# P times V of every fourth key tile as three f16 products, with P split into f16 halves on Pool

## The chip, the cores and the metric

One core of a Trainium2 chip runs the whole layer. The metric is the device time of one launch in microseconds; a smaller one is better. The core has a matrix engine (TensorE, PE in the profile; its weight loads are listed apart as PEld), a vector engine (VectorE, DVE), a scalar engine with activation functions (ScalarE, ACT), a general engine (GpSimd, POOL) and an engine that issues transfers (SyncE, SP). Each runs its own list of instructions in order, and waits on semaphores for the others. Matmul results go to PSUM, of which the kernel uses eight banks of 128 x 512 f32.

## The reference

A transformer block over S = 2048 rows of D = 512, in f32. `mod` holds six rows, `c` being a single conditioning vector.

```python
mod = (_silu(c) @ w_mod).reshape(c.shape[0], 6, 1, -1)
sa, ca, ga, sb, cb, gb = ...
h = _layernorm(x, axis=-1) * (1 + ca) + sa
x = x + ga * _A_ref(h, A_wq, A_wk, A_wv, A_wo)      # 32 query heads of 16, one key and one value head
h = _layernorm(x, axis=-1) * (1 + cb) + sb
x = x + gb * _B_ref(h, B_w_gate, B_w_up, B_w_down)  # ((h Wg) * (h Wu)) Wd, F = 1792
```

In the attention, scores = q k / 4, p = softmax(scores) over 2048 keys, and o = p v. No mask is used.

## The kernel before, in words

**Units and turns.** Attention is cut into 32 units: 8 strips of 256 rows times 4 groups of 8 heads. A unit runs through 16 key tiles of 128 keys. For a key tile, four score products (`qk_exp`, L659, or L657 where the product is issued in two pieces of 256) give 128 keys x 512 (two heads times 256 rows) in a PSUM bank each; ACT takes the exponential of each into an f32 tile P (L661). The row maximum that the exponent needs is folded into the products as an extra row of q, and comes from a separate pass one unit earlier (`max_mm`: products `mx`, L601, reduced by DVE, L605). So in each turn PE makes four products `sc` for ACT and four products `mx` for DVE.

**P times V.** `pv(u, kt)` (L670) multiplies the four P tiles of a key tile by `vst[:, kt, :]`: 16 columns of V, and 16 of ones that sum the softmax. The four products use 32 columns of the array each and run side by side; all are f32. They go to one bank for the 16 key tiles of a unit, which `pv_out` scales and copies out (L676). `end_turn` issues the burst for the key tile of the turn before, so that each turn ends in one burst of four f32 products.

**Side work.** All other products are f16. Where f32 accuracy is wanted, an operand is split into a high and a low f16 half, and three products (high x high, low x high, high x low: `TERMS`) are summed. Score products, maxima and side products use only half of the array's rows, and run in pairs on the two halves. The side work is the q projection (`q_proj`), the output projection (`wo_work`), gate and up (112 groups, 14 for each strip), and down (two groups for each strip). `attend` orders a pair of turns by a string: `NO_SIDE` where no side work is open, `FEW` (four side steps per turn) in the q projections of the first units, and `MANY` (eight per turn) later: x is a step of side work, m a maximum, e a score product, and the figure is the half of the array. The burst and the ends follow the string.

**The guard.** In one turn all side steps use one half of the array, in the next turn the other, but both halves of a group add into one PSUM bank. `Group.half` therefore puts a dependence on the first side step of a turn: it waits for the exponential that followed the last side step of the turn before (`sync`). In `MANY` the last score product comes after the last side step, so that this is the fourth exponential of the turn; and the side step that waits is the first product of the new turn, in front of all others on PE's queue.

**Pool's work.** Pool splits operands into f16 halves: the two halves of the gate-up product after each group (L850, L851), the attention output (L706 to L709), and h2T (L818, L819). Up to some 474 us it also scales and splits the FFN weights, one slice per 1.25 turns or so: three instructions each (L1079 to L1081 for gate and up, L1073, L1080, L1081 for down). `hooks` hands them out by a count of steps, two to a turn, not by Pool's progress.

Of the kernel before, what the change touches and what calls it, by code (L numbers as in the profile page):

```python
# [33 lines left out]
ROW_LAG = 4  # L34
SLOTS = (0, 1, 2, 3, 6, 7)
SUM_GAP = 4.0
# [4 lines left out]
NORM_AT = (5, 12, 15, 19)  # L41
NBANK = 8
QPRE = 24
Q_LAG = 8
# [19 lines left out]
def adaln_mqa_glu_kernel(ctx: ExitStack, tc: tile.TileContext, x_in, wq_in, wk_in, wv_in, wo_in,  # L64
# [160 lines left out]
    hfs = kwb[:, 0:2 * NHF * BT].bitcast(F32).rearrange("p (n t) -> p n t", n=NHF)  # L225
    ssqs = [kwb[:, 2 * n * BT:2 * n * BT + 2 * F].bitcast(F32) for n in (KC, 2 * KC)]
    kng = kwb[:, 2 * NHF * BT:2 * NHF * BT + BT]

# [85 lines left out]
    def v_mm(b):  # L314
        p = ps_hold("pvt", (128, 4, 16))
        for i in range(4):
            nc.tensor.matmul(p[:, i, :], parts[b][:, i * 128:(i + 1) * 128], lane[:, 16:32], start=True, stop=True)

        def out():
            nc.scalar.activation(vst[:, 4 * b:4 * b + 4, 0:16], p, AF.Copy, scale=inv[:, 0:1] if b else 1.0)  # L320
            ps_give(p)
        posts.append(out)
# [47 lines left out]
    q_part(0, 0)  # L370
    kb = consts.tile([128, 8], F32, name="kb")
    inv = consts.tile([128, 3], F32, name="inv")
    fwd = consts.tile([128, 3], F32, name="fwd")
# [13 lines left out]
    nc.vector.tensor_scalar(hsb, modT[0][:, :, 0:64:32], fwd[:, 0:1], None, op0=OP.mult)  # L387
    nc.gpsimd.tensor_scalar(sckb, sck, inv[:, 0:1], 0.0, op0=OP.mult, op1=OP.add)
    combine(0, selk)
    combine((0, 0), selq)  # L390
# [7 lines left out]
    ln_norm(1, (None, nc.scalar, None, nc.scalar))  # L398
    evs = consts.tile([128, 1], F32, name="evs")

    def ev_scales():

        t = work.tile([128, 2], F32, name="evt", bufs=1)
        nc.vector.tensor_reduce(evs, ident.rearrange("p (a r) -> p a r", a=4)[:, :, 0:16], axis=AX.XY, op=OP.add)
        nc.vector.reciprocal(t[:, 0:1], kb[:, 5:6])
        nc.gpsimd.tensor_tensor(t[:, 0:1], t[:, 0:1], evs, op=OP.mult)
        nc.gpsimd.tensor_scalar(t[:, 1:2], evs, -1.0, 1.0, op0=OP.mult, op1=OP.add)
        nc.gpsimd.tensor_tensor(evs, t[:, 0:1], t[:, 1:2], op=OP.add)

    qvs = consts.tile([128, 1], F32, name="qvs")  # L410
# [42 lines left out]
    def last_rows():  # L453
# [20 lines left out]
             12: lambda: (k_evac(3), h_halves(3, KA)), 13: lambda: h_halves(3, KB),  # L474
             15: lambda: h_halves(1, KA), 17: lambda: h_halves(1, KB), 20: ev_scales}
    later_h = deque((2, k) for k in range(KC))
# [164 lines left out]

    pvb = {}
    ptl = {}
    oc = {}
    och = {}
    pd = {}

    def qk_exp(u, kt, p, a, last=False):
        s = sst[u % 3]
        ptl[u, kt, p, a] = work.tile([128, D], F32, name="P", tag="P", bufs=8)  # L650
        t = ps_sc()
# [6 lines left out]
        else:  # L658
            nc.tensor.matmul(t.rearrange("k (c n) -> k c n", c=2), keys, s[64 * a:64 * a + 50, :, p, :],  # L659
                             start=True, stop=True)  # L660
        ex = nc.scalar.activation(ptl[u, kt, p, a], t, AF.Exp)  # L661
        if sync["due"]:
            sync.update(due=False, exp=ex.ins.name)

    def pv(u, kt):
        if kt == 0:
            pvb[u] = ps_hold("pv")
        for j in range(4):
            p, a = divmod(j, 2)
            nc.tensor.matmul(pvb[u][32 * j:32 * j + 32, :], vst[:, kt, :], ptl[u, kt, p, a],  # L670
                             start=(kt == 0), stop=(kt == KT - 1))
# [120 lines left out]
    def ln2_work(sb):  # L792
        st = {}

        def tr(i):
            def f():
                if not h2s:
                    h2T = big.tile([128, 2, 2, KC, ST], F16, name="h2T", tag="wq")
                    glus.append(big.tile([128, 2, 2, FT, ST], F16, name="glu", tag="big"))
                    h2s.update({s: h2T[:, s % 2] for s in range(NS)})  # L800
# [31 lines left out]
    def ffn_work(sb):  # L832

        def glu():
            return glus[0][:, sb % 2]

# [56 lines left out]
    def late_weights():  # L893
# [37 lines left out]
        def stage(n):  # L931
            if "d" in W:
                t = work.tile([128, D], F32, name="wsl", tag="xl", bufs=3)
            else:
                t = hfs[:, SLOTS[taken[0] % len(SLOTS)], :]
                taken[0] += 1
# [281 lines left out]
    def attend(u, kt):  # L1218
# [6 lines left out]
        style = NO_SIDE if side is None else FEW if side in few else MANY  # L1225
        orders = [[(w[0], int(w[1:] or 0)) for w in s.split()] for s in (style if style is NO_SIDE else (style, style))]
        count = {}

        def end_turn(kt):
# [3 lines left out]
            for f in ends:  # L1233
                f()
            ends.clear()
            v = u * KT + kt - 1
# [76 lines left out]

    pv(u, KT - 1)
    pv_out(u)
    sync["before"] = sync["exp"]
# [60 lines left out]
```

## Time and profile before

| what | value |
|---|---|
| median of three runs | 1665.11 us (1664.57 to 1665.29) |
| span of the profiled execution | 1663.8 us |
| PE busy | 1643.3 us, 99% of the span |
| DVE busy | 1402.3 us, 84% |
| ACT busy | 1234.8 us, 74% |
| POOL busy | 523.5 us, 31% |

The profiled execution has only a span, from the first to the last instruction; it is 1.3 us below the median of the timed runs. A row of the timeline gives the start, the length, the engine, the line, the operation, the tiles (out<-in), how many instructions the row merges, and in brackets how long the engine sat idle before it, and what ended that. A row of the groups gives after the count the busy time of the group and the mean length of one instruction in ns. A row of the windows gives for each engine the busy us and in brackets the number of instructions, and then the granted TensorE clock as a share of full speed.

### The profile page before, as it was taken

Reading aid. Unit: us, or ns where it says so; the run is one execution under the profiler, and the core shown is the slowest. Engines: PE = TensorE matmul, PEld = TensorE weight load, DVE = VectorE, ACT = ScalarE, POOL = GpSimd, SP = SyncE. Lnnn points to the kernel's source line nnn. Section 1 sums busy time; section 2 is a strip of 40 time slices with the busy share of each in tenths; the row PEclk is TensorE's granted clock in tenths of the full one; section 3 lists DMA queues with packets and bytes.
Section 4 is the critical chain, followed back from the end, with each engine's and each line's share of the span. In section 5 each row is a group of like instructions: output and inputs, shape, how many; then the busy total and the mean of one; then the engine's idle time right before and its main releaser. Section 6 shows DMA issues by size and latency. Waiting matters only on the chain.

```text
span 1663.8 us, 39821 instructions
## 1 busy us (share of the span) xinstructions
PE 1643.3 (99%) x15677; PEld 747.1 (45%) x15677; DVE 1402.3 (84%) x2434; ACT 1234.8 (74%) x2389; POOL 523.5 (31%) x833
## 2 busy tenths in 40 slices
PE   8899999999999999999999999999999999999999
PEld 4333333355533554335543355434545345454776
DVE  7999999998998999899998999999998999980211
ACT  5688888888777877777877787777878777877300
POOL 4857537864841111301112011300113001210322
PEclk9999999999999999999999999999999999999999
DMA  6313313342210001000000000000000000000100
GB/s 237 108 59 100 95 43 120 96 129 80 77 51 24 18 12 32 19 32 20 20 26 23 25 13 24 26 25 26 20 29 15 26 22 20 26 14 21 33 13 14
DMA packets 66024, 75.39 MB, mean 45 GB/s; under 512 B 17702, under 2 KB 46634, under 8 KB 65836
## 3 DMA queue, kind: packets, MB, share of 16 engines
q1 hardware_dynamic: 63724, 72.26, 13.7%
q8 instruction: 123, 2.02, 0.5%
q10 hardware_dynamic: 2112, 0.59, 0.1%
q14 instruction: 65, 0.53, 0.1%
HBM read 55.51 MB, written 17.04 MB: 44 GB/s over the span
## 4 chain that ended last, share of the span: by engine, by line
PE 93%; ACT 2%; DVE 2%; DMA 1%; issue 1%; POOL 0%; SPq 0%; ACTq 0%; DVEq 0%
PE side L511 41%; PE pv L670 30%; PE mx L601 8%; PE sc L659 8%; PE sc L657 3%; ACT P L661 2%; DVE mpart L605 1%; DMA xbig<-in_A_x_dram 1%; PE mx L805 1%; PE mxt L629 0%; ACT hf L813 0%; PE sc L601 0%; DVE bs L248 0%; DMA kwb<-in_B_w_down_dram 0%; DMA wkv<-in_A_wv_dram 0%
## 5 line engine op out<-in xcount | busy, mean ns | idle before, releaser
L605 DVE TENSOR_REDUCE mpart<-mx 128x1 f32<-128x512 f32 x2016 | 1274.1, 684 | 104.0 <-PE mx L601 95.7
L661 ACT ACTIVATE P<-sc 128x512 f32<-128x512 f32 x2048 | 1094.8, 598 | 274.2 <-PE sc L659 226.9
L601 PE MATMUL mx<-kst,sst 48*128 48x512 f16 x2032 | 631.5, 377 | 3.8 <-ACT P L661 1.7
L659 PE MATMUL sc<-sst,kst 50*128 50x512 f16 x1792 | 597.5, 379 | 0.6 <-ACT P L661 0.3
L670 PE MATMUL pv<-P,vst 128*32 128x512 f32 x4096 | 545.3, 605 | 0.7
L511 PE MATMUL side<-h2T,wg 64*128 64x256 f16 (+1 forms) x2396 | 540.8, 271 | 0.1
L511 PE MATMUL side<-h2T,wu 64*128 64x256 f16 (+1 forms) x2396 | 538.7, 270 | 0.0
L511 PEld LDWEIGHTS <-wg 64*128 64x128 f16 (+1 forms) x2396 | 226.0, 94 | 230.5 <-ACT P L661 194.0
L511 PE MATMUL side<-wd,glu 64*128 64x512 f16 (+1 forms) x1172 | 272.8, 378 | 0.2 <-ACT P L661 0.2
L850 POOL TENSOR_SCALAR glu<-gf 128x256 f16<-128x256 f32 x112 | 45.8, 409 | 671.3 <-DVE gf L849 583.9
L511 PEld LDWEIGHTS <-wu 64*128 64x128 f16 (+1 forms) x2396 | 226.4, 94 | 43.0 <-issue 7.8
L601 PEld LDWEIGHTS <-sst 48*128 48x128 f16 x2064 | 189.9, 94 | 34.2 <-issue 17.4
L659 PEld LDWEIGHTS <-kst 50*128 50x128 f16 x1792 | 162.9, 94 | 63.0 <-issue 50.3
L511 PEld LDWEIGHTS <-glu 64*128 64x128 f16 (+1 forms) x1172 | 98.5, 94 | 192.4 <-ACT P L661 85.9
L670 PEld LDWEIGHTS pv<-P,vst 128*32 128x32 f32 x4096 | 80.7, 108 | 160.9 <-issue 150.1
L849 DVE TENSOR_TENSOR gf<-side,g 128x256 f32<-128x256 f32 x112 | 46.7, 418 | 79.8 <-ACT g L847 77.7
L657 PE MATMUL sc<-sst,kst 50*128 50x256 f16 x512 | 96.9, 268 | 0.1
L511 PE MATMUL side<-h,wq 64*128 64x512 f16 (+1 forms) x372 | 95.0, 376 | 0.4 <-ACT P L661 0.4
L847 ACT ACTIVATE g<-side 128x256 f32<-128x256 f32 x112 | 42.3, 379 | 65.6 <-PE side L511 65.3
L511 PE MATMUL side<-wo,och 64*128 64x512 f16 (+1 forms) x360 | 86.3, 377 | 0.0
L851 POOL TENSOR_TENSOR glu<-gf,glu 128x256 f16<-128x256 f32 x112 | 75.3, 673 | 9.3
L706 POOL TENSOR_TENSOR oc<-oc,rr 128x256 f32<-128x256 f32 x31 | 22.7, 731 | 146.6 <-DMA rr<-ri 100.4
(233 smaller groups left out, 865.4 us busy)
## 6 DMA issues: line engine op xcount, KB each, us to landing
pd<-ev SPq DMA_DIRECT2D x32, 256.0 KB
kwb<-in_B_w_gate_dram SPq DMA_DIRECT2D x32, 224.0 KB
kwb<-in_B_w_up_dram SPq DMA_DIRECT2D x32, 224.0 KB
sst<-qd SPq DMA_DIRECT2D x180, 32.0 KB
qd<-q SPq DMA_DIRECT2D x16, 256.0 KB
oc<-pd SPq DMA_DIRECT2D x64, 64.0 KB
rr<-ri SPq DMA_DIRECT2D x64, 64.0 KB
x<-in_A_x_dram SPq DMA_DIRECT2D x14, 256.0 KB
```

The lines of the kernel that those rows point to most:

```text
L511: return nc.tensor.matmul(self.p[:, c * w:(c + 1) * w], left[rows], right[rows], start=start and c == 0, stop=stop and c == len(terms) - 1)
L601: nc.tensor.matmul(m, s[64 * a:64 * a + 48, t // 2, p, t % 2 * 128:(t % 2 + 1) * 128], w[64 * a:64 * a + 48, :], start=(i == 0), stop=(i = ...
L605: nc.vector.tensor_reduce(part, m, axis=AX.X, op=OP.max)
L657: nc.tensor.matmul(t[:, c * ST:(c + 1) * ST], keys, s[64 * a:64 * a + 50, c, p, :], start=True, stop=True)
L659: nc.tensor.matmul(t.rearrange("k (c n) -> k c n", c=2), keys, s[64 * a:64 * a + 50, :, p, :], start=True, stop=True)
L661: ex = nc.scalar.activation(ptl[u, kt, p, a], t, AF.Exp)
L670: nc.tensor.matmul(pvb[u][32 * j:32 * j + 32, :], vst[:, kt, :], ptl[u, kt, p, a], start=(kt == 0), stop=(kt == KT - 1))
L706: eng.tensor_tensor(o, o, st["r"], op=OP.mult)
L847: nc.scalar.activation(g, p[:, 0:ST], AF.Copy, scale=2.0 ** -45)
L849: nc.vector.tensor_tensor(gf, p[:, ST:2 * ST], g, op=OP.mult)
L850: nc.gpsimd.tensor_scalar(glu()[:, 0, f, :], gf, 1.0, 0.0, op0=OP.mult, op1=OP.add)
L851: nc.gpsimd.tensor_tensor(glu()[:, 1, f, :], gf, glu()[:, 0, f, :], op=OP.subtract)
```

## The change

In `MANY` turns, every fourth key tile (kt = 0, 4, 8, 12) is now a split tile, once the space for it exists (it lies behind the gate-up halves, in a place that is free from the sixth unit on). Its four P tiles are written into one of two sets; Pool makes a high and a low half of each (`p_halves`, two instructions per P tile, one P tile per turn, at the turn's end); and its part of P times V is three f16 products for each P tile, with V split once into `v16`. The burst of a split tile is kept back until the next split tile is due, which is four turns later. At the end of a unit, what is kept back follows the last f32 burst at once. To keep P and V in the range of f16, all exponentials now get a bias of 14 ln 2 from a 128 x 1 tile (`pbias`), and V is scaled by `vsc` when it is stored; the scaling in `pv_out` falls away. The gate-up halves have one buffer instead of two, and two of the six staging slots of the weights lie elsewhere.

```diff
-SLOTS = (0, 1, 2, 3, 6, 7)
+SLOTS = (0, 1, 2, 3, 12, 13)
+EVERY = 4
+P_BIAS = float(14 * np.log(2.0))
...
+    pbias = consts.tile([128, 1], F32, name="pbias")
+    nc.gpsimd.memset(pbias, P_BIAS)
+    v16 = consts.tile([128, 2, KT // EVERY, 32], F16, name="v16")
...
     def qk_exp(u, kt, p, a, last=False):
...
-        ptl[u, kt, p, a] = work.tile([128, D], F32, name="P", tag="P", bufs=8)
+        if (u, kt) in split_p:
+            ptl[u, kt, p, a] = p_sets[split_p[u, kt]][0][:, 2 * a + p]
+            todo_p.append((u, kt, p, a))
+        else:
+            ptl[u, kt, p, a] = work.tile([128, D], F32, name="P", tag="P", bufs=8)
...
-        ex = nc.scalar.activation(ptl[u, kt, p, a], t, AF.Exp)
+        ex = nc.scalar.activation(ptl[u, kt, p, a], t, AF.Exp, bias=pbias)
...
+    def p_halves():
+        if todo_p:
+            u, kt, p, a = todo_p.popleft()
+            hi, lo = p_view(split_p[u, kt], 2 * a + p)
+            t = ptl[u, kt, p, a]
+            nc.gpsimd.tensor_scalar(hi, t, 1.0, 0.0, op0=OP.mult, op1=OP.add)
+            nc.gpsimd.tensor_tensor(lo, t, hi, op=OP.subtract)
+
     def pv(u, kt):
...
+        for n, (vl, pl) in enumerate(((0, 0), (1, 0), (0, 1))):
+            for j in range(4):
+                p, a = divmod(j, 2)
+                nc.tensor.matmul(pvb[u][32 * j:32 * j + 32, :], v16[:, vl, kt // EVERY, :],
+                                 p_view(split_p[u, kt], 2 * a + p)[pl], start=start and n == 0, stop=stop and n == 2)
+
+    def pv_turn(u, kt):
+        if (u, kt) in split_p:
+            late_p.append((u, kt))
+            if len(late_p) > 1:
+                pv(*late_p.popleft())
+        else:
+            pv(u, kt)
+        if kt == KT - 1:
+            while late_p:
+                pv(*late_p.popleft())
+            ends.append(lambda: pv_out(u))
...
-        nc.scalar.activation(ev, pvb[u], AF.Copy, scale=evs)
+        nc.scalar.activation(ev, pvb[u], AF.Copy)
...
+        if style is MANY and kt % EVERY == 0 and p_sets:
+            split_p[u, kt] = len(split_p) % 2
...
         def end_turn(kt):
...
+            p_halves()
             v = u * KT + kt - 1
             if v >= 0:
-                pv(*divmod(v, KT))
-                if v % KT == KT - 1:
-                    ends.append(lambda: pv_out(u - 1))
+                pv_turn(*divmod(v, KT))
```

In the built program 105 of the 512 key tiles are split tiles, the first of them the last of the sixth unit, and Pool has 420 pairs of new instructions. Three places show how the instructions move.

On Pool, in the sixth unit, where the first split tile comes. `kwb`, `wu` and `wg` are the FFN weights being split, `gf` a gate-up product, and `glu` is the tile that holds both the gate-up halves and, new, the P sets. Before:

```order
L1079 TENSOR_SCALAR kwb<-kwb,sca 128x448
L1080 TENSOR_SCALAR wu<-kwb 128x448
L1081 TENSOR_TENSOR wu<-kwb,wu 128x448
L1079 TENSOR_SCALAR kwb<-kwb,sca 128x448
L1080 TENSOR_SCALAR wu<-kwb 128x448
L1081 TENSOR_TENSOR wu<-kwb,wu 128x448
L1079 TENSOR_SCALAR kwb<-kwb,sca 128x448
```

and now, from the same first row on:

```order
L1129 TENSOR_SCALAR kwb<-kwb,sca 128x448
L1130 TENSOR_SCALAR wu<-kwb 128x448
L1131 TENSOR_TENSOR wu<-kwb,wu 128x448
L680 TENSOR_SCALAR glu<-glu 128x512
L681 TENSOR_TENSOR glu<-glu 128x512
L680 TENSOR_SCALAR glu<-glu 128x512
L681 TENSOR_TENSOR glu<-glu 128x512
L1129 TENSOR_SCALAR kwb<-kwb,sca 128x448
L1130 TENSOR_SCALAR wu<-kwb 128x448
L1131 TENSOR_TENSOR wu<-kwb,wu 128x448
L680 TENSOR_SCALAR glu<-glu 128x512
L681 TENSOR_TENSOR glu<-glu 128x512
```

One pair L680, L681 now stands in Pool's queue for every turn from here to the last unit's end, between the slices of the weights, which keep their places by steps.

On PE, at the end of a unit (`sc` is a score product, `side` a side group, here of gate and up). Before, the burst is four f32 products, and the first weight load of the next turn waits for ACT:

```order
L657 MATMUL sc_5277<-sst0_128,kst_132 128x256
L670 MATMUL pv_4542<-P_5154,vst_126 32x512
L670 MATMUL pv_4542<-P_5198,vst_126 32x512
L670 MATMUL pv_4542<-P_5168,vst_126 32x512
L670 MATMUL pv_4542<-P_5220,vst_126 32x512
L511 LDWEIGHTS wg_4055 [waits Activation_49]
```

and now twelve f16 products stand behind the four, of which these are the first:

```order
L667 MATMUL sc_5276<-sst0_128,kst_132 128x256
L692 MATMUL pv_4541<-P_5151,vst_126 32x512
L692 MATMUL pv_4541<-P_5197,vst_126 32x512
L692 MATMUL pv_4541<-P_5165,vst_126 32x512
L692 MATMUL pv_4541<-P_5219,vst_126 32x512
L700 LDWEIGHTS v16_341
L700 MATMUL pv_4541<-glu_4878,v16_341 32x512 [waits Pool_49]
```

The f16 products wait for Pool. They end as the f32 ones do, in front of a weight load that waits for ACT.

On PE, one turn later (the turn of kt = 1 of a unit): the burst that stood there is gone, and the weight load that waits for ACT follows the score product directly.

```order
L509 LDWEIGHTS wu_4055
L509 MATMUL side_5202<-h2T_4877,wu_4055 128x256
L667 LDWEIGHTS kst_132
L667 MATMUL sc_5341<-sst0_128,kst_132 128x256
L509 LDWEIGHTS wg_4054 [waits Activation_49]
L509 MATMUL side_5202<-h2T_4877,wg_4054 128x256
```

More of the change, by code (lines that the diff above doesn't have):

```diff
@@ L319, in out @@
         def out():
-            nc.scalar.activation(vst[:, 4 * b:4 * b + 4, 0:16], p, AF.Copy, scale=inv[:, 0:1] if b else 1.0)
+            nc.scalar.activation(vst[:, 4 * b:4 * b + 4, 0:16], p, AF.Copy, scale=vsc[:, 1:2] if b else vsc[:, 0:1])
             ps_give(p)
@@ L388, in adaln_mqa_glu_kernel @@
     nc.gpsimd.tensor_scalar(sckb, sck, inv[:, 0:1], 0.0, op0=OP.mult, op1=OP.add)
+    nc.vector.reciprocal(vsc[:, 0:1], kb[:, 5:6])
+    nc.gpsimd.tensor_tensor(vsc[:, 1:2], vsc[:, 0:1], inv[:, 0:1], op=OP.mult)
     combine(0, selk)
@@ L398, in adaln_mqa_glu_kernel @@
     ln_norm(1, (None, nc.scalar, None, nc.scalar))
[L399 to L408, printed above, removed]
     qvs = consts.tile([128, 1], F32, name="qvs")
@@ L642, in adaln_mqa_glu_kernel, with p_view @@
     pvb = {}
+    did_pv = {}
     ptl = {}
+    split_p = {}
+    p_sets = []
+    todo_p = deque()
+    late_p = deque()
+    def p_view(n, j):
+        return [p_sets[n][1][:, j, h] for h in range(2)]
     oc = {}
```

41 lines of the change are left out of this document (29 added, 12 removed).

## The prediction

> **What bounds the kernel now.** I read the page first, then the groups, then the timeline of single turns, and last Pool by windows.
>
> ```profile
> span 1663.8 us, 39821 instructions
> PE 1643.3 (99%) x15677; PEld 747.1 (45%) x15677; DVE 1402.3 (84%) x2434; ACT 1234.8 (74%) x2389; POOL 523.5 (31%) x833
> POOL 4857537864841111301112011300113001210322
> PE 93%; ACT 2%; DVE 2%; DMA 1%; issue 1%; POOL 0%; SPq 0%; ACTq 0%; DVEq 0%
> L661 ACT ACTIVATE P<-sc 128x512 f32<-128x512 f32 x2048 | 1094.8, 598 | 274.2 <-PE sc L659 226.9 <-PE mx L601 30.6 <-PE side L511 3.1
> L670 PE MATMUL pv<-P,vst 128*32 128x512 f32 x4096 | 545.3, 605 | 0.7
> ```
>
> PE is busy throughout and carries 93% of the chain that ended last, so whatever shortens or lengthens PE's list moves the end. Pool's 31% is a mean over unlike stages: in the first eleven slices (to 458 us) it stands at 3 to 8 tenths, afterwards mostly at 1.
>
> Two turns in the timeline, one with side steps of down and one of gate and up, show how close ACT runs behind PE:
>
> ```profile
> 900.77 1.06 PE L670 MATMUL pv<-P,vst 128*32 128x512 f32 x8
> 901.77 0.39 PE L511 MATMUL side<-wd,glu 64*128 64x512 f16 x1
> 902.00 0.38 PE L511 MATMUL side<-wd,glu 64*128 64x512 f16 x1
> 902.21 0.38 PE L511 MATMUL side<-wd,glu 64*128 64x512 f16 x1
> 902.23 2.17 ACT L661 ACTIVATE P<-sc 128x512 f32<-128x512 f32 x4 [0.67 <-PE sc L659]
> 903.61 1.07 PE L670 MATMUL pv<-P,vst 128*32 128x512 f32 x8
> 904.60 0.09 PEld L511 LDWEIGHTS <-glu 64*128 64x128 f16 x1 [0.84 <-ACT P L661]
> ...
> 945.29 2.12 ACT L661 ACTIVATE P<-sc 128x512 f32<-128x512 f32 x4 [0.71 <-PE sc L659]
> 946.64 1.06 PE L670 MATMUL pv<-P,vst 128*32 128x512 f32 x8
> 947.63 0.09 PEld L511 LDWEIGHTS <-wg 64*128 64x128 f16 x1 [0.84 <-ACT P L661]
> ```
>
> A turn is 2.84 us (900.77 to 903.61). A burst holds PE for 1.00 (900.77 to 901.77), and a pair of side and score products 0.21. The four exponentials end at 904.40, and the next turn's first weight load, which must wait for the fourth, comes at 904.60. In the gate-up turn it is 947.41 and 947.63. How short that can get shows in a turn in which ACT was late:
>
> ```profile
> 1339.80 1.57 ACT L661 ACTIVATE P<-sc 128x512 f32<-128x512 f32 x3 [0.18 <-PE sc L659]
> 1340.39 1.10 PE L670 MATMUL pv<-P,vst 128*32 128x512 f32 x8
> 1341.42 0.09 PEld L511 LDWEIGHTS <-glu 64*128 64x128 f16 x1 [0.84 <-ACT P L661]
> ```
>
> ACT ended at 1341.37 and the load came 0.05 later, at 1.03 after the burst's start. So the guard has 0.20 - 0.05 = 0.15 us to spare in a down turn and 0.17 in a gate-up turn. PE is the bound, with ACT 0.15 us behind it in every turn.
>
> **The shorter burst.** A pass of 512 columns is 0.21 us (902.00 to 902.21). I take an f32 product as four such passes, as 1.00 for the burst suggests, so that three f16 products make a burst of about 0.78 and 105 of them save 23 us if PE may go on. It may not: the guard lets it go on only 0.15 to 0.17 earlier. The turn whose burst is moved away gains no more than that, since the load that waits for ACT now follows the last score product directly. At a unit's end the kept-back burst is then added to an f32 one, at 3 x 0.21 = 0.64, say 0.65 with its loads, where nothing covers it. Per unit that is 4 x -0.16 + 0.65, or nothing; of the gain nothing is left even if all else stood still.
>
> **The bias on the exponentials.** It was an immediate zero and is now a 128 x 1 tile. The trace of before has such operands elsewhere on ACT:
>
> ```profile
> L301 ACT ACTIVATE hi<-pk,sck 128x512 f16<-128x512 f32 x4 | 2.8, 690 | 0.1
> L301 ACT ACTIVATE hi<-pk,rows,sckb 128x512 f16<-128x512 f32 x3 | 2.3, 781 | 0.0
> 26.91 2.79 ACT L270 ACTIVATE kwb<-sc,hsb 128x512 f32<-128x512 f32 x4 [0.81 <-PE sc L267]
> 180.69 2.07 ACT L661 ACTIVATE P<-sc 128x512 f32<-128x512 f32 x4 [0.69 <-PE mx L601]
> 182.81 0.23 PEld L511 LDWEIGHTS <-wq 64*128 64x128 f16 x2
> 182.94 0.38 PE L511 MATMUL side<-h,wq 64*128 64x512 f16 x1
> ```
>
> With none 598 ns (L661), with one 690, with two 781: 0.09 us for each. It also holds ACT: four exponentials back to back take 2.07, a spacing of (2.07 - 0.60)/3 = 0.49; four with two such operands take 2.79, (2.79 - 0.78)/3 = 0.67. With one I take 0.58, and four exponentials take 3 x 0.58 + 0.69 = 2.43. That is 0.26 more than 2.17 and 0.31 more than 2.12. Less what the guard has to spare, PE waits 0.11 to 0.14 in a turn. I take 0.09, because 2.17 and 2.12 hold waits for score products that don't grow. Bounds: 0.03, if most of the added time falls into those waits, and 0.15. In the early q turns the load came at 182.81, 0.05 after ACT's end, but its product could only start at 182.94, so that 0.13 is spare: 2.43 - 2.07 - 0.13 = 0.23, and I take 0.20.
>
> Counting bursts in the timeline, the one at 324.67 is the 92nd of 512 and the one at 478.09 the 144th. Of the first 92 turns some 70 are q turns, of which I count 60 as tight: 12 us, and 22 x 0.09 = 2. Of the 366 from the 144th on, the 23 with a double burst are covered by it; 343 x 0.09 = 31.
>
> The Trainium skill, page "ScalarE: Activation LUTs", section "What ACT_TABLE_LOAD costs", gives 186 ns + 0.833 ns per element, 93 ns more for each 128 x 1 operand, and an overlap of 93 ns back to back. By it the exponential would have 706 ns at a spacing of 613, four would take 2.55, and an estimate from it is 0.12 more in each of some 425 turns, or 1830 us for the whole. The trace is shorter at the same form (598 against its 613, spacing 0.49 against 0.52), so I stay with the rows.
>
> **Pool.** Each turn with split tiles gives Pool one pair: a tensor_scalar and a tensor_tensor on 128 x 512. The down weights' split (L1080, L1081) has the same two forms.
>
> ```profile
> 329.05 0.64 POOL L1079 TENSOR_SCALAR kwb<-kwb,sca 128x448 f32<-128x448 f32 x1
> 439.63 0.62 POOL L1080 TENSOR_SCALAR wd<-wsl 128x512 f16<-128x512 f32 x1
> 440.33 1.16 POOL L1081 TENSOR_TENSOR wd<-wsl,wd 128x512 f16<-128x512 f32 x1
> 441.45 1.27 POOL L1073 TENSOR_TENSOR wsl<-wsl,gbb 128x512 f32<-128x512 f32 x1
> 324.67 1.06 PE L670 MATMUL pv<-P,vst 128*32 128x512 f32 x8
> 478.09 1.06 PE L670 MATMUL pv<-P,vst 128*32 128x512 f32 x8
> 329.05:479.40 150.35, 148.52 (x1586) 73.79 (x1582) 136.61 (x234) 123.62 (x253) 102.04 (x136) 1.00 0.30 89
> ```
>
> From 439.63 to 441.45 the pair holds Pool for 1.82 us. By the order the first pair now stands where L1079 began at 329.05. From there to 479.40 Pool has 102.0 us of old work, and some 67 of its steps wait 0.08 for the one before (0.62 after 439.63 is 440.25, the next starts at 440.33): 107. The turns 92 to 143 add 52 x 1.82 = 94.6. Pool thus needs 201.6 us where 150.4 are there. The four turns' delay lets Pool be late, but only by two turns before the burst needs the last pair, and at a unit's end by one. PE waits for Pool burst by burst, and Pool never waits for PE in that stretch, so its work sets the time: the low half for the burst of turn 144 is ready at 329.05 + 201.6 = 530.7 and is needed 1.3 after that burst's start (0.90 of f32 and two f16 passes), which puts the burst at 529.4 instead of 478.1: **+51**. The exponentials' 0.09 doesn't add here. Bounds: 47 (two turns' more lateness is borne) and 56 (weights' loads delayed, since SP waits for staging slots that Pool empties later; behind such a load stand q, P-out and row-maximum transfers). From there on a turn's Pool work falls to 1.82 + 0.37 for gate-up halves, under 2.9, and Pool catches up.
>
> In that stretch 18 pairs more (33 us) would not fit either. DVE isn't slowed by a busy Pool: the maxima took 684 ns from 424 to 476 us, where Pool was busy for 45 of 52 us, and 685 from 900 to 945, where the slices show Pool at 0 to 2 tenths.
>
> ```profile
> L605 DVE TENSOR_REDUCE mpart<-mx 128x1 f32<-128x512 f32 x74 | 46.9, 684 | 4.1 <-PE mx L601 3.9
> L605 DVE TENSOR_REDUCE mpart<-mx 128x1 f32<-128x512 f32 x64 | 40.5, 685 | 3.8 <-PE mx L601 3.8
> 424.00:476.00 52.00, 52.00 (x518) 22.11 (x510) 47.91 (x82) 41.11 (x80) 45.08 (x50) 1.00 0.29 82
> ```
>
> At nothing I cost the copy-out without its scale, `vsc` (one reciprocal on DVE for two small operations saved), the moved staging slots (SP's list keeps its order) and the single gate-up buffer (a strip's down groups end before the next strip's first gate group); without that cover each would cost 1 us or less.
>
> **Sum.** Exponentials before the split 14 (6 to 20), Pool 51 (47 to 56), exponentials after it 31 (10 to 55), double bursts 24 x 0.65 = 16 (12 to 18), a cold clock after Pool's last wait 2 (0 to 5): 114. On the profiled execution that is 1663.8 + 114 = 1777.8; the median lies 1.3 above its span, so **1779**. The ends add to 75 and 154: 1740 to 1819.
>
> **Rivals.**
> - *Pool's lateness is borne by the four turns' delay and the bias is hidden*, so the passes are saved: 105 x 0.22 = 23, 1642. This needs a pair under (150.4 - 107)/52 = 0.83 us against 1.82 in the rows. 0.02.
> - *The bias costs nothing*, because its read overlaps. Then the turns gain 0.16 four times per unit and the double burst gives it back; Pool's 51 and 2 stay: 1718. The 690 against 598 speaks against it. 0.08.
> - *Pool keeps up, the bias holds ACT*: 14 + 392 x 0.09 + 26 x 0.65 = 66, 1731. 0.04.
> - *PE loses its clock in the waits for Pool.*
>
> ```profile
> 50.00:55.00 5.00, 3.41 (x18) 1.76 (x19) 4.94 (x9) 3.45 (x7) 4.75 (x8) 1.00 0.00 0
> 55.00:60.00 5.00, 4.37 (x22) 2.02 (x23) 5.00 (x12) 3.08 (x6) 4.75 (x6) 0.53 0.00 0
> 60.00:65.00 5.00, 5.00 (x30) 1.98 (x26) 5.00 (x19) 4.61 (x10) 4.75 (x7) 0.79 0.01 3
> ```
>
> After PE had idled 1.6 of 5 us, the granted clock fell to 0.53 and 0.79 of full speed in the next ten, which at half speed is 6.8 us, and costs 3.4. Between two split bursts PE needs 4 x 2.93 = 11.7 and Pool 201.6/13 = 15.5: one such stretch is covered, two make 18.5 and cost 3.0 in each of 13 gaps: +39, 1818. The Trainium skill, page "TensorE: Matmul & The Clock Gate", section "What's actually happening", has half speed after an idle window of about 3.4 us; by that rule only the longer waits count, and one stretch per gap at most. The trace's shorter idling sufficed once. 0.06.
>
> **Chances.** The forecast has 0.80. The range 1740 to 1819 holds it and the last rival, and leaves out the other three (0.14) and a little of its own tails. A difference under 0.2% (3 us) can't be told from none here. Faster 0.02 (the first rival), same 0.01, slower 0.97.
>
> **What would show it.** Right: exponentials of 690 ns; from about 340 to 540 us Pool at 9 tenths, with PE waiting for P's halves and the burst of the 144th turn some 65 us late (14 + 51); later turns of 2.93, with weight loads 0.05 after ACT's end; bursts of 1.6 us at unit ends. Wrong: exponentials of 598; no wait of `pv` for Pool; turns with an f16 burst 0.2 shorter than the others.

## The result, and the profile after

The changed kernel takes 1796.55 us (median of five runs, 1793.93 to 1798.86), the kernel before in the same session 1665.29: a ratio of 1.0787, 95% interval 1.0774 to 1.08. It is slower by 131 us; the prediction was 1779. The profiled execution has a span of 1794.5 us, 130.7 above that of before.

The page and the groups of after, the same lines as shown of before:

```profile
span 1794.5 us, 42056 instructions
PE 1681.5 (94%) x16097; PEld 769.9 (43%) x16097; DVE 1409.1 (79%) x2433; ACT 1383.3 (77%) x2389; POOL 1264.8 (70%) x1674
POOL 5756638999997677776778666776778767776532
PE 55%; ACT 23%; POOL 12%; issue 5%; DVE 3%; DMA 1%; ACTq 0%; POOLq 0%; SPq 0%; DVEq 0%
L671 ACT ACTIVATE P<-sc,pbias 128x512 f32<-128x512 f32 x1628 | 1006.2, 692 | 122.4 <-PE sc L669 101.4
L692 PE MATMUL pv<-P,vst 128*32 128x512 f32 x3256 | 434.5, 605 | 0.8 <-ACT P L671 0.8
L700 PE MATMUL pv<-glu,v 128*32 128x512 f16 x1260 | 97.7, 386 | 32.0 <-POOL glu L680 25.5
```

PE had 93% of the chain before. Now it has 55%, ACT 23% and Pool 12%. An exponential has 692 ns where it had 598. In the slices, Pool stands at 9 tenths from the eighth to the twelfth, 314 to 538 us, and after that mostly at 6 to 8, where it had 0 to 3. The f16 bursts (L700) waited 32 us for Pool in all.

Two turns of after in the timeline, with side steps of gate and up:

```profile
956.19 1.07 PE L692 MATMUL pv<-P,vst 128*32 128x512 f32 x8
957.74 2.43 ACT L671 ACTIVATE P<-sc,pbias 128x512 f32<-128x512 f32 x4 [0.54 <-PE sc L669]
959.17 1.06 PE L692 MATMUL pv<-P,vst 128*32 128x512 f32 x8
960.22 0.09 PEld L509 LDWEIGHTS <-wg 64*128 64x128 f16 x1 [0.89 <-ACT P L671]
```

The four exponentials take 2.43 us, as worked out, and end at 960.17; the weight load comes 0.05 later. Burst to burst it is 2.98, where a turn of before had 2.84 (900.77 to 903.61 in the prediction's timeline). The 0.15 us by which ACT ran behind PE are used up, and ACT sets the pace. At a unit's end the f16 burst that was kept back follows the f32 one:

```profile
888.79 1.07 PE L692 MATMUL pv<-P,vst 128*32 128x512 f32 x8
889.67 0.83 PE L700 MATMUL pv<-glu,v 128*32 128x512 f16 x12
890.43 0.09 PEld L509 LDWEIGHTS <-wg 64*128 64x128 f16 x1 [0.42 <-issue]
```

From the first burst to the next turn's load it is 1.64 us, where one burst of before took 1.00.

Pool by windows, in the stretch in which it cannot keep up (the granted clock is the last number but two):

```profile
341.60:547.50 205.90, 169.53 (x1641) 80.43 (x1641) 137.44 (x232) 139.51 (x252) 193.36 (x240) 0.92 0.21 65
```

Pool is busy for 193 of 206 us, and the rest is the 0.09 us or less between its instructions, so it never rests. One wait of PE in that stretch, in the timeline of Pool and of the bursts (`glu` holds the P sets; L680 and L681 are a pair of halves, L1123, L1130 and L1131 a slice of the down weights):

```profile
488.90 1.27 POOL L1123 TENSOR_TENSOR wsl<-wsl,gbb 128x512 f32<-128x512 f32 x1
489.54 0.40 PE L700 MATMUL pv<-glu,v 128*32 128x512 f16 x3
490.25 0.62 POOL L1130 TENSOR_SCALAR wd<-wsl 128x512 f16<-128x512 f32 x1
490.96 1.15 POOL L1131 TENSOR_TENSOR wd<-wsl,wd 128x512 f16<-128x512 f32 x1
...
493.20 0.62 POOL L680 TENSOR_SCALAR glu<-glu 128x512 f16<-128x512 f32 x1
493.88 0.88 PE L700 MATMUL pv<-glu,v 128*32 128x512 f16 x8 [3.95 <-POOL glu L680]
493.91 1.15 POOL L681 TENSOR_TENSOR glu<-glu 128x512 f16<-128x512 f32 x1
```

PE starts the first three products of its burst at 489.54 and then waits 3.95 us, while Pool finishes a weight slice and gate-up halves and only then makes the next high half.

To place the 130.7 us I took the start of each turn's first exponential in both traces and subtracted. This difference is called the shift, and the experiments below are read the same way:

| turn | 0 | 92 | 144 | 146 | 256 | 511 | span |
|---|---|---|---|---|---|---|---|
| after minus before, us | 1.5 | 11.0 | 64.0 | 67.0 | 82.1 | 126.7 | 130.7 |

The prediction had 14 at the 92nd turn and 65 at the 144th (burst at 542.07 against 478.09: 64). The miss lies behind that: 60 us from turn 146 to 511, where it had 47.

### The profile page after: what moved, and what is told of

Read it like the earlier page. It is cut to its first block, busy times and chain, and to the rows that moved or that the text cites. A ratio compares the mean times of both kernels' runs of the same rounds, so it can differ in the third digit from the quotient of the medians.

```text
span 1794.5 us, 42056 instructions
## 1 busy us (share of the span) xinstructions
PE 1681.5 (94%) x16097; PEld 769.9 (43%) x16097; DVE 1409.1 (79%) x2433; ACT 1383.3 (77%) x2389; POOL 1264.8 (70%) x1674
## 4 chain that ended last, share of the span: by engine, by line
PE 55%; ACT 23%; POOL 12%; issue 5%; DVE 3%; DMA 1%; ACTq 0%; POOLq 0%; SPq 0%; DVEq 0%
PE side L509 27%; ACT P L671 15%; PE pv L692 12%; PE sc L669 7%; ACT glu L671 7%; PE mx L599 5%; POOL glu L681 3%; DVE mpart L603 2%; POOL glu L680 2%; PE sc L667 1%; PE pv L700 1%; POOL wd L1131 1%; POOL wsl L1123 1%; POOL wu L1131 1%; POOL glu L901 1%
## 5 line engine op out<-in xcount | busy, mean ns | idle before, releaser
L671 ACT ACTIVATE P<-sc,pbias 128x512 f32<-128x512 f32 x1628 | 1006.2, 692 | 122.4 <-PE sc L669 101.4
L599 PE MATMUL mx<-kst,sst 48*128 48x512 f16 x2032 | 642.1, 380 | 4.5 <-DVE sst L307 1.0
L509 PE MATMUL side<-h2T,wg 64*128 64x256 f16 (+1 forms) x2396 | 550.9, 273 | 27.1 <-ACT P L671 21.7
L509 PE MATMUL side<-h2T,wu 64*128 64x256 f16 (+1 forms) x2396 | 553.4, 273 | 0.0
L681 POOL TENSOR_TENSOR glu<-glu 128x512 f16<-128x512 f32 x420 | 486.7, 1159 | 35.0
L692 PE MATMUL pv<-P,vst 128*32 128x512 f32 x3256 | 434.5, 605 | 0.8 <-ACT P L671 0.8
L671 ACT ACTIVATE glu<-sc,pbias 128x512 f32<-128x512 f32 x420 | 266.3, 685 | 129.3 <-PE sc L669 113.8
L680 POOL TENSOR_SCALAR glu<-glu 128x512 f16<-128x512 f32 x420 | 260.7, 621 | 97.5 <-PE mx L599 67.7
L509 PEld LDWEIGHTS <-glu 64*128 64x128 f16 (+1 forms) x1172 | 100.2, 95 | 205.9 <-ACT P L671 98.8
L700 PE MATMUL pv<-glu,v 128*32 128x512 f16 x1260 | 97.7, 386 | 32.0 <-POOL glu L680 25.5
L692 PEld LDWEIGHTS pv<-P,vst 128*32 128x32 f32 x3256 | 64.6, 108 | 129.0 <-issue 120.4
```

Source lines behind the costliest of these rows:

```text
L509: return nc.tensor.matmul(self.p[:, c * w:(c + 1) * w], left[rows], right[rows], start=start and c == 0, stop=stop and c == len(terms) - 1)
L599: nc.tensor.matmul(m, s[64 * a:64 * a + 48, t // 2, p, t % 2 * 128:(t % 2 + 1) * 128], w[64 * a:64 * a + 48, :], start=(i == 0), stop=(i = ...
L671: ex = nc.scalar.activation(ptl[u, kt, p, a], t, AF.Exp, bias=pbias)
L680: nc.gpsimd.tensor_scalar(hi, t, 1.0, 0.0, op0=OP.mult, op1=OP.add)
L681: nc.gpsimd.tensor_tensor(lo, t, hi, op=OP.subtract)
L700: nc.tensor.matmul(pvb[u][32 * j:32 * j + 32, :], v16[:, vl, kt // EVERY, :], p_view(split_p[u, kt], 2 * a + p)[pl], start=start and n == ...
```

## The experiments

The theory is the prediction's sum: the bias costs what ACT's longer exponentials leave PE waiting; Pool's total work sets the time up to the 144th turn; and from there on the split gives and takes nothing but the double burst. Rivals: that the bias and Pool's lateness hide one another, that PE's waits and its halved clock (and not Pool's total) make the loss, and that the f16 bursts cost something in themselves. All are compared with the kernel before on the same chip. The diffs show the core of each edit.

### Bias, Pool's early work, and neither

Four kernels take the bias, Pool's early work, or both away, or add the bias alone. Without the bias, P keeps its plain scale.

After without the bias:

```diff
-        ex = nc.scalar.activation(ptl[u, kt, p, a], t, AF.Exp, bias=pbias)
+        ex = nc.scalar.activation(ptl[u, kt, p, a], t, AF.Exp)
```

> The changed kernel with one operand less: the exponentials have no bias again, so P is 2^14 times smaller; all else stays, the Pool pairs and the kept-back bursts too. Theory (three separate costs: the bias through the guard, Pool's overload, the double burst): exponentials of 598 ns; no shift before the first split tile (11 us with the bias); Pool's stretch still costs 51 to 56 by the 144th turn; after it nothing, since four turns of a unit gain 0.16 each and the double burst takes 0.65 back: 1718 to 1724. Rival (the later turns are longer because of Pool's and the P sets' traffic, not because of the bias): only the 11 us before the split go, 1785.

Measured: 1737.25 us (1736.81 to 1739.28), ratio 1.0431 (1.0416 to 1.0445). The bias is worth 59 us of the 131, and 13 us more remain than the theory has.

The kernel before with the bias alone, on f32 products throughout:

```diff
-        ex = nc.scalar.activation(ptl[u, kt, p, a], t, AF.Exp)
+        ex = nc.scalar.activation(ptl[u, kt, p, a], t, AF.Exp, bias=pbias)
```

> The kernel before with one operand more: the exponentials get the 128 x 1 bias, so that P is 2^14 times larger and the ratio the same; no split, no Pool pairs. Theory: 11 us by the 92nd turn as in the changed kernel, then 0.12 in each of the other 420 turns: 61 in all, 1726 (1710 to 1735). Rival (the bias matters in the early turns alone, the rest of the lengthening comes with the split): 1676.

Measured: 1724.99 us (1723.42 to 1725.71), ratio 1.0353 (1.0339 to 1.0367). The group of the exponentials in this kernel:

```profile
L664 ACT ACTIVATE P<-sc,pbias 128x512 f32<-128x512 f32 x2048 | 1245.5, 689 | 194.8 <-PE sc L662 167.9 <-PE mx L604 11.1 <-PE side L514 9.8
```

One operand on one line costs 59 us, without a single split tile. The shift rises to 9.4 by turn 92 and then by 0.115 per turn to 57.6.

After, with the split only from the tenth unit on, when the weights are done:

```diff
-        if style is MANY and kt % EVERY == 0 and p_sets:
+        if style is MANY and kt % EVERY == 0 and p_sets and u >= 9:
```

> The changed kernel with the first split tile in the tenth unit instead of the sixth (81 or more split tiles less 13): by then Pool has split all FFN weights. Bias and double bursts stay. Theory: Pool has 1.82 + 0.37 us of work for turns of 3, so no overload: the 56 us of Pool's stretch shrink to the bias's 0.12 in 52 turns, and three double bursts go: 1796 - 56 + 6 - 2 = 1744. Rival (PE's waits for Pool would come in any stretch, since the pairs themselves are late by a turn at a unit's end): over 1770.

Measured: 1744.64 us (1743.32 to 1746.44), ratio 1.0473 (1.0459 to 1.0488). It still has 92 of the 105 split tiles and is 52 us below after: that is Pool's early work.

Both edits together:

> Both together: no bias, and split tiles from the tenth unit on (23 units, 92 tiles). What is left of the change is f16 products, Pool pairs and kept-back bursts. Theory: the guard lets PE go on 0.16 earlier at four turn ends of a unit, the double burst costs 0.65: 23 x (0.65 - 0.64), the time of before within 4 us, 1661 to 1669. Rival 1 (the shorter bursts are worth their passes, 0.22 each, and the turn without burst its 1.00): 23 x (0.65 - 3 x 0.22 - 0.9) = -21, 1644. Rival 2 (Pool's work alone lengthens turns): over 1675.

Measured: 1679.44 us (1678.44 to 1682.5), ratio 1.0084 (1.007 to 1.0098). The theory had no difference from before, and this is a miss by 10 us or more; the time lies where the second rival had it. The shift shows that it isn't the turns in general that grow. From turn 146 to turn 256 it falls by 0.7 in all, so a plain unit does come out at nothing, as the prediction had it: 0.82 more at the double burst, and 0.28 to 0.35 less in each of the four turns whose burst is an f16 one or missing. But in three units it jumps by 4.1, 4.1 and 2.6. The timeline at the first jump (L855 are the four transposes of a row tile for the second layer norm, L811 is the normalisation of that tile, which Pool does in strips 2 to 5):

```profile
884.88 0.73 POOL L748 TENSOR_TENSOR oc<-oc,rr 128x256 f32<-128x256 f32 x1
886.62 0.33 PE L855 MATMUL mx<-ident,n 128*128 128x128 f32 x1
886.85 2.07 POOL L811 TENSOR_SCALAR n<-x,st,ry 128x512 f32<-128x512 f32 x1
888.98 0.55 PE L855 MATMUL mx<-ident,n 128*128 128x128 f32 x3 [2.03 <-POOL n L811]
```

PE waits 2.03 us for an instruction that now stands in Pool's queue behind pairs of halves and the attention output. In the kernel before it was done 2.6 us ahead of the transposes (there L769 and L805):

```profile
880.80 2.07 POOL L769 TENSOR_SCALAR n<-x,st,ry 128x512 f32<-128x512 f32 x1
885.51 0.66 PE L805 MATMUL mx<-ident,n 128*128 128x128 f32 x4
```

The wait stands in after too, 1.43, 1.22 and 1.21 us long:

```profile
971.72 2.07 POOL L811 TENSOR_SCALAR n<-x,st,ry 128x512 f32<-128x512 f32 x1
973.85 0.55 PE L855 MATMUL mx<-ident,n 128*128 128x128 f32 x3 [1.43 <-POOL n L811]
```

### The double burst, the transposes' wait, and Pool's work by itself

The next runs test these readings, starting from the kernel without bias and with the late start.

First the kept-back burst of a unit's last split tile is carried into the next unit, to its first split slot, and the unit is copied out after it:

```diff
+    def pv_late():
+        u, kt = late_p.popleft()
+        pv(u, kt)
+        if did_pv[u] == KT:
+            ends.append(lambda: pv_out(u))
...
         else:
             pv(u, kt)
-        if kt == KT - 1:
+            if kt == 0 and late_p:
+                pv_late()
+        if kt == KT - 1 and u == NU - 1:
             while late_p:
                 pv(*late_p.popleft())
+        if kt == KT - 1 and not late_p:
             ends.append(lambda: pv_out(u))
```

> After without the exponentials' bias and with the split only from unit 9 on, and the last f16 burst of a unit is not flushed beside the unit's last f32 burst but carried into the next unit's first split slot (the output copy of the unit follows it). Theory: the double burst costs 0.65 to 0.85 us at the end of each of some 23 units and the moved slots are free, so 15 to 19 us go from the 1679.4 of the same kernel with double bursts: 1660 to 1665. Rival: the emptied slot, and not the second burst in one gap, is what costs, or a burst has the same price wherever it stands: 1677 to 1681.

Measured: 1663.58 us (1661.6 to 1664.47), ratio 0.9988 (0.9979 to 0.9997). The 0.82 at the unit's first turn is 0.05 now, and a plain unit gains 0.68 on before: the four times 0.16 that the prediction let the double burst eat. The jumps stay, and so do their waits. The first of them in the timeline (the transposes are L864 here, the normalisation L820):

```profile
883.37 0.90 PE L864 MATMUL mx<-ident,n 128*128 128x128 f32 x3 [2.06 <-POOL n L820]
```

Right behind it the clock is halved, as the windows ahead of, in and behind that stretch show:

```profile
881.00:883.30 2.30, 0.31 (x5) 0.12 (x1) 0.35 (x1) 0.00 (x0) 2.30 (x3) 1.00 0.00 0
883.30:886.70 3.40, 3.33 (x15) 1.38 (x17) 0.80 (x2) 2.39 (x5) 3.15 (x5) 0.50 0.00 0
886.70:890.00 3.30, 3.30 (x29) 1.19 (x26) 2.26 (x4) 1.84 (x5) 3.13 (x5) 1.00 0.01 2
```

Such a jump is thus 2 us of wait and 3.4 us at half speed, which cost 1.7.

Then, with the double bursts kept, the normalisation goes to ACT in all strips:

```diff
-        on_pool = 2 <= sb < NS - 2
+        on_pool = False
```

> After without the bias and with the split from unit 9 on, double bursts kept; the row normalisation of strips 2 to 5 runs on ACT, as that of the other strips does, instead of on Pool (L811, 2.07 us each, x8). Theory: the three steps of about 4 us at the strip boundaries come from TensorE's transposes (L855) waiting for that instruction, which now queues behind pairs of halves on Pool, and from the half clock behind the wait; without it 8 to 12 us go from 1679.4: 1667 to 1671. Rival: the transposes wait for other work of the strip (its sums on Pool or DVE), and the step stays: 1677 to 1681.

Measured: 1670.15 us (1669.77 to 1672.73), ratio 1.0033 (1.0021 to 1.0044): 9.3 us below the same kernel with the work on Pool. The jumps are 0.9, 1.1 and 0.6, and no transpose waits. So it was that wait.

Pool's work by itself, in after without the bias and with its early start: all pairs are formed at the same places, from the finished V, and no product reads them; P times V is four f32 products in every turn, as before the change.

```diff
-            t = ptl[u, kt, p, a]
+            t = vst.rearrange("p k c -> p (k c)")
             nc.gpsimd.tensor_scalar(hi, t, 1.0, 0.0, op0=OP.mult, op1=OP.add)
             nc.gpsimd.tensor_tensor(lo, t, hi, op=OP.subtract)
...
-        if (u, kt) not in split_p:
+        if True:
             for j in range(4):
```

> After without the bias, in which Pool still forms all its pairs of halves at the same places, reading the finished V in place of P, and nobody reads what it forms: all products of P and V are four f32 matmuls in the slots of the kernel before. The output is that of f32 products; what is left out is the use of the halves. Theory: it is Pool's total work in the first third (LN2, glu and weight halves queued behind the pairs) that makes the start late, not TensorE's wait for a pair of halves as such, so most of the 57.8 us between after without bias (1737.25) and the same with a late start (1679.44) stays, and the strip boundaries' 12: 1715 to 1735. Rival: the loss is made by TensorE's waits at the f16 bursts (some 25 us, with some 17 us of half clock behind them), and goes when no burst waits: 1675 to 1695.

Measured: 1727.41 us (1726.9 to 1731.43), ratio 1.0379 (1.0365 to 1.0393). By turn 144 the shift is 54.5, of which 1.2 was there at the start: what after has there without its bias (55.5). No burst waits for a pair in this kernel. The list of PE's waits from 325 to 545 us shows who waits instead:

```profile
PE side L509 <- POOL wd L1122: 14.6, 6, 4.5
PE mx L599 <- ACT P L670: 10.2, 6, 2.8
PE sc L666 <- DVE mpart L603: 5.5, 2, 5.3
PE side L509 <- POOL wd L1123: 4.3, 6, 0.8
```

Down products wait for weights that Pool has not split yet. Where PE waits is exchangeable; that Pool has more work than time until the weights are done is not.

### Putting the pieces together

Without bias, with late start, carried bursts and the normalisation on ACT, and with 14 ln 2 taken off the row maximum, so that P has the scale of after without an operand on the exponential:

```diff
         nc.vector.tensor_reduce(mms[u], mparts[u], axis=AX.X, op=OP.max)
+        nc.vector.tensor_scalar(mms[u], mms[u], -P_BIAS, None, op0=OP.add)
```

> All of it together: no bias on the exponentials, but 14 ln 2 taken off the rows' maximum by one small VectorE instruction per unit, so that P has the scale of after; split from unit 9 on; last f16 burst of a unit carried into the next; row normalisation on ACT. Theory: the gains add, 1679.4 - 15 to 19 (carried bursts) - 8 to 12 (normalisation) + 0 to 2 (32 small instructions) = 1648 to 1658, below the kernel before, because four f16 bursts a unit are 0.16 us shorter each. Rival: what is late next (ACT's exponentials) takes the gain away: 1663 to 1668.

Measured: 1666.52 us (1664.24 to 1669.66), ratio 1.0006 (0.9997 to 1.0015). A miss by 9 us. PE's waits name the suspect; L621 is the new VectorE instruction, L628 the transpose of the row maxima:

```profile
PE mxt L628 <- DVE mm L621: 4.9, 12, 0.9
```

In the mean of units 9 to 30 the shift grows by 0.21 and 0.20 us more in turns 13 and 14 of a unit than in the kernel with the carried bursts. Two runs separate this from the normalisation: everything but that instruction, and the carried bursts with that instruction alone.

> The kernel with everything together (1666.52) without the small VectorE instruction that takes 14 ln 2 off the maximum, so P keeps its plain scale: no bias, split from unit 9 on, carried bursts, row normalisation on ACT. Theory: that instruction lies on the way from the maximum's last block to TensorE's transpose of the row maxima (L628), and its cost showed in turns 13 and 14 of each unit, 0.26 and 0.22 us more than with the carry alone, 32 times: 10 to 14 us go, 1653 to 1657. Rival: the miss of that kernel came from the normalisation on ACT together with the carry, whose gains don't add: 1663 to 1667.

Measured: 1653.92 us (1652.32 to 1655.18), ratio 0.9927 (0.9915 to 0.994).

> The kernel with the carried bursts (1663.58) plus the small VectorE instruction that takes 14 ln 2 off each unit's maximum, row normalisation on Pool as in after. Theory: the instruction costs 0.3 to 0.45 us per unit, 10 to 14 us in all: 1673 to 1678. Rival: it lies beside other work and costs nothing: 1663 to 1666.

Measured: 1674.84 us (1673.62 to 1675.65), ratio 1.0055 (1.0042 to 1.0069). The small instruction costs 12.6 us in one pair of kernels (1666.52 - 1653.92) and 11.3 in the other (1674.84 - 1663.58), and the normalisation on ACT gains 9.7 (1663.58 - 1653.92) with the carried bursts, 9.3 without. The kernels of these differences ran on different chips; taken against the kernel before on each chip (1665.31, 1666.23 and 1666.0) they are 13.5, 10.3, 10.6 and 8.6, so each is good to 1 or 2 us. Within that the gains do add. What failed was the small instruction. It takes 0.45 us in the mean (x32), where nothing disturbs it 0.17, and stands between the maximum and the transpose that PE waits for. PE's waits for it make 4.9 us; how the rest of the loss in turns 13 and 14 comes about is open. Its group in the kernel with the carried bursts and this instruction alone:

```profile
L621 DVE TENSOR_SCALAR mm<-mm 128x16 f32<-128x16 f32 x32 | 14.5, 452 | 1.1
```

What disturbs it is in the last section.

The kernel of 1653.92 us is below both kernels of this case. Its timeline shows the turns that gain:

```profile
896.45 1.07 PE L692 MATMUL pv<-P,vst 128*32 128x512 f32 x8
899.29 0.83 PE L700 MATMUL pv<-glu,v 128*32 128x512 f16 x12
901.97 1.06 PE L692 MATMUL pv<-P,vst 128*32 128x512 f32 x8
904.92 1.06 PE L692 MATMUL pv<-P,vst 128*32 128x512 f32 x8
```

From the f32 burst to the f16 one it is 2.84; from the f16 burst to the next 2.68; the turn after it takes 2.95 and gives part of it back. Whether P without the factor of 2^14 has the precision that is wanted is a question apart from its time.

## Why the prediction was right, and where it was off

The forecast, and not a rival, is what happened: 1796.55 in a range of 1740 to 1819, with each of the three mechanisms found by itself. Term by term, with the shifts of after and of the experiments:

| term | predicted, us | measured, us | from |
|---|---|---|---|
| exponentials before the split | 14 (6 to 20) | 9.5 | after, turn 0 to 92; bias alone 9.6 |
| Pool overload | 51 (47 to 56) | 53 at turn 144, 56 at 146 | after; at turn 144 55 without bias, 53 for the pairs alone |
| exponentials after turn 144 | 31 (10 to 55) | 42 | bias alone, 57.6 - 15.2 from turn 146 |
| double bursts | 16 (12 to 18) | 11 | 2.38 per plain unit in after less 1.89 with the bias alone, x 22.8 units |
| strip boundaries | not seen | 4.5 | three turns with the wait, 1.6 each in after, less 0.0 to 0.1 with the bias alone |
| end | 2 (0 to 5) | 4.0 | span less turn 511 |

With the 1.5 at turn 0, whose cause was not looked for, and 56 for Pool the measured terms make 128.5, of 130.7; 2 us are not placed.

**The bias.** The length (692 against 690) and the four in a row (2.43) came as worked out. The working gave 0.11 to 0.14 per turn, and I then took 0.09, "because 2.17 and 2.12 hold waits for score products that don't grow". That step failed: with the bias alone a turn lost 0.115, so nearly nothing of the added time fell into those waits. It is 11 us. The other deviations lie between 5 below and 5 above their terms and add to 3.5; that they nearly cancel is luck. The early q turns were charged 0.20 each and cost 0.12, (9.5 - 22 x 0.115)/60. The estimate from the Trainium skill's page "ScalarE: Activation LUTs", section "What ACT_TABLE_LOAD costs", 1830 us, was 33 too high. The trace agrees with the page's 93 ns per operand (692 - 598 = 94), and the spacing of four in a row, (2.43 - 0.69)/3 = 0.58, is again under the 613 that the page's formula gives.

**Pool.** Pool's work counted out, 201.6 us from where the first pair stands, came within 5 us. That the exponentials add nothing in this stretch is borne out too: from turn 92 to 146 after loses 55.9 us, and after without the bias 58.7. The step "its work sets the time" is shown by the pairs alone: 53 us with nobody waiting for them. The step "PE waits for Pool burst by burst" describes after, but isn't what makes the loss.

**The clock.** The last rival wasn't wrong on the fact. In the stretch of 205.9 us the granted clock was 0.92 in the mean, which is (1 - 0.92) x 205.9 / 0.5 = 33 us at half speed. One of these stretches, behind a wait of 4.25 us at 507.6:

```profile
506.00:511.00 5.00, 1.60 (x15) 0.52 (x12) 2.53 (x4) 2.31 (x4) 4.75 (x6) 1.00 0.37 95
511.00:516.00 5.00, 3.97 (x21) 1.19 (x22) 0.71 (x2) 1.50 (x3) 4.75 (x6) 0.52 0.20 52
516.00:521.00 5.00, 5.00 (x38) 1.25 (x34) 3.67 (x6) 3.10 (x6) 4.66 (x7) 0.80 0.16 52
```

The run with the pairs alone doesn't settle this rival, since its clock falls too (to 0.92 in the mean from 440 to 500 us, and 0.77 from 500 to 545). What does is Pool's list: in after, and in the pairs alone from 325 to 545 us, no gap between two Pool instructions is over 0.09 us, so Pool's own instructions fill the time, and PE's slow products only filled time in which it would have waited. The rival's 39 us needed the half clock to reach beyond Pool's work, and it did not.

**The double burst.** It costs 0.80 to 0.85 at the unit's first turn, not 0.65. Against it stand, without the bias, the four turns of -0.28 to -0.35; the turns in between give part of that back, and the net of 0.68 per unit that the carried bursts brought out is close to the 4 x 0.16 of the prediction. With the bias a part of that gain is there as well, so that the net is 0.49 per unit (2.38 - 1.89) and not the 0.65 of the sum.

**What was not seen.** For the later turns the prediction said that Pool catches up, 1.82 + 0.37 under 2.9 per turn. That holds in the mean. It left out the 2.07 us of the row normalisation, for which PE waits at a strip's boundary: one long instruction with a deadline, in a queue that is now two thirds full. In after the wait is 1.2 to 1.4 us with no halved clock behind it, and makes 4.5 us. Without the bias it is 2 us, in most cases with a halved clock behind it, and makes 9: the three jumps of 4.1, 4.1 and 2.6 us shrink to 0.9, 1.1 and 0.6 when ACT does the work, and the time by 9.3. That the wait is longer there is measured; that the longer turns of after give Pool the time to be less late is argued only.

**The end.** In after the last kept-back burst stands behind two f32 bursts and waits twice more for Pool, 0.57 and 0.62 us, and 3.4 us at half clock follow. No run was made for this term; of the kernels without the bias those with f16 bursts lose 2.2 there and the one without them nothing.

**The other rivals.** That the bias costs nothing was to give 1718, and after without it takes 1737.25; that Pool keeps up was to give 1731, and after with the late start takes 1744.64. Each is some 14 to 19 us short, for the reasons above: both lack the strip boundaries, and the second also the larger price of the bias per turn. That the lateness is borne and the bias hidden is ruled out by both runs.

## What to carry to other kernels

Where two engines run 0.15 us apart in every turn, an operand that makes one instruction of the follower 16% longer becomes a term of its own: count four of them a turn, 512 turns, before asking what the product gains. An idle engine on the page (Pool's 31%) may still have little room in one stretch of the program (102 of 150 us were taken) and hold a few instructions with a deadline in the rest; sum its work by stage, and list who waits for it, before giving it more. And a moved burst gains only if it lands in a slot that is empty: the same four f16 bursts were worth nothing when one of them doubled up, and 0.68 us per unit when it was carried on.

## What the runs showed of the hardware

- **The clock after short waits.** Five kernels without the bias leave the normalisation on Pool (both starts, the pairs alone, and the carried bursts with and without the small instruction). Each has three waits for it, of 1.7 to 2.1 us, and ten of these fifteen waits were followed by 3.4 us at half clock. Those of 1.43, 1.22 and 1.21 us in after, and the waits of 0.9 us in its turns, were not. The traces show what separates them. The stretches at half clock of a run start whole multiples of 3.413 us apart: with the carried bursts at 883.29, 1071.02 and 1258.75, which is 55 times 3.413 each. I cut the eight traces with such stretches behind 100 us into windows on this grid, and took PE's busy time in each. Of the windows at full clock, all 31 in which PE was busy for less than 48.5% were followed by half clock, 4 of the 30 between that and 67%, and none of the 3633 above. Two waits in the kernel with the carried bursts and the small instruction, 1.97 and 1.98 us long, each with the window in which most of it lies, and the next:

```profile
1075.54:1078.95 3.41, 1.69 (x20) 1.31 (x22) 0.57 (x2) 1.10 (x3) 3.33 (x3) 1.00 0.01 2
1078.95:1082.37 3.42, 3.34 (x36) 1.73 (x34) 2.19 (x5) 2.62 (x6) 3.25 (x6) 1.00 0.02 5
1263.28:1266.69 3.41, 1.43 (x17) 1.16 (x19) 0.57 (x2) 0.85 (x2) 3.33 (x3) 1.00 0.00 0
1266.69:1270.10 3.41, 3.41 (x23) 1.10 (x19) 2.27 (x4) 2.23 (x5) 3.24 (x6) 0.50 0.02 5
```

  With 1.69 us busy of 3.41 the clock stayed, with 1.43 it fell. So it is not the length of a wait alone that counts, but how much of one window it empties. Where between 48% and 67% the border lies, and whether busy time is the right measure, these traces leave open. The Trainium skill, page "TensorE: Matmul & The Clock Gate", section "What's actually happening", has windows of about 3.4 us that run freely, whatever the kernel does. The grid agrees with that; a window needn't be idle, as the prediction took it from there, but half empty was enough here.
- **A small VectorE instruction waits for Pool's running one.** The instruction that shifts the maximum (128 x 16, L621) takes 0.17 us when Pool is idle or done within that time. In 21 of its 32 places in the kernel with the carried bursts and this instruction it ended some 0.03 us after the Pool instruction that ran at its start, and took up to 1.04. Two of the 32 places, the first beside a pair of halves (L681, L682), the second with Pool idle:

```profile
706.40 0.22 DVE L620 TENSOR_REDUCE mm<-mpart 128x16 f32<-128x64 f32 x1
706.41 1.16 POOL L682 TENSOR_TENSOR glu<-glu 128x512 f16<-128x512 f32 x1
706.65 0.94 DVE L621 TENSOR_SCALAR mm<-mm 128x16 f32<-128x16 f32 x1
707.74 0.27 PE L628 MATMUL mxt<-ident,mm 128*16 128x128 f32 x1 [0.60 <-DVE mm L621]
...
798.92 0.22 DVE L620 TENSOR_REDUCE mm<-mpart 128x16 f32<-128x64 f32 x1
799.18 0.17 DVE L621 TENSOR_SCALAR mm<-mm 128x16 f32<-128x16 f32 x1
```

  Pool's instruction ends at 707.57 and DVE's at 707.59; PE has idled 0.60 by then. The reduction ahead of it takes 0.22 both times, though Pool starts 0.01 behind it at 706.41, and the maxima (683 ns, out of PSUM) are as fast with Pool at 70% as they were with Pool at 31%. So the prediction's "DVE isn't slowed by a busy Pool" holds for the maxima, from which it was read, and not for this form. The Trainium skill, page "GPSIMD Engine Reference", section "8. Key points", names contention of the two engines for DVE instructions in a 2-port mode or with two SBUF inputs. This instruction has one SBUF input, and no run here shows in which mode it ran. What the runs show for this form, SBUF to SBUF in f32, is contention of the kind that isn't a slower rate but a wait for the end of Pool's instruction.
